# A dense layer with GELU, forward and backward: a shorter identity matrix, first loads on other queues, and all lists of operations written anew

## The chip, the core and the metric

The kernel runs on one core of a Trainium2 chip. A core has a matrix engine (TensorE, PE in the profile; its weight loads are shown apart as PEld), a vector engine (VectorE, DVE), a scalar engine (ScalarE, ACT), a general engine (GpSimd, POOL), and SyncE (SP), which here only issues transfers. Transfers run on 16 DMA engines. The metric is the device time of one execution in microseconds; three executions of the kernel before took 265.57 to 265.78 us, with a median of 265.76 us.

## What is computed

The reference is the forward pass and all gradients of a two-layer block with S = 2048 rows, D = 448 and F = 1792, in bf16:

```
h   = gelu_tanh(x @ w1 + b1)          # 2048 x 1792
out = h @ w2 + b2                     # 2048 x 448
gh  = (g @ w2.T) * gelu_tanh'(x @ w1 + b1)
gx  = gh @ w1.T    gw1 = x.T @ gh     gb1 = sum over rows of gh
gw2 = h.T @ g      gb2 = sum over rows of g
```

The outputs are out, gx, gw1, gb1, gw2 and gb2.

## The kernel before, in words

The rows are cut into 4 blocks of 512 and the 1792 hidden columns into 7 pairs of 128-column tiles, so there are 28 units called pairs, p = 0 to 27 (block p // 7). For a pair, TensorE makes `u` = x @ w1 (operations `u{p}.1` and `u{p}.2`, the two directions in which 64-row halves of the array are paired) and `q` = g @ w2.T (`q{p}.1`, `q{p}.2`). Between them and the results stand, for each pair: two copies of u out of PSUM with the bias added (`c{p}A`, `c{p}B`, on ScalarE or VectorE), the GELU and the square on ScalarE (`g`, `s`), six operations on VectorE (`e`, `r`, `y`, `z`, `m`, `n`) around a tanh on ScalarE (`t`), and last `G{p}` on VectorE, which multiplies by q and writes gh. There is one pair of PSUM banks for q, so q of the next pair waits for `G` of this one. The units `p`, `o` and `x` are the products h @ w2 and gh @ w1.T: `p{c}.{i}` makes a part of block 0's output from pair c, and `o{b}.{half}.{f0}.{f1}.{d}` and `x{b}.{half}.{f0}.{f1}.{d}` make half of block b over the hidden tiles f0 to f1. Their results are taken from PSUM by `vo` and `vx` on VectorE or ScalarE. After the last block come gw1 (line 775) and gw2 (line 829), each a run of full 128-row matmuls.

The order on each engine is written out by hand in `PE_ORDER`, `ACT_ORDER`, `DVE_ORDER` and `SP_ORDER`; a `Plan` links readers with writers and emits each engine's list in that order, so an engine that waits holds up all that is behind it. `UB` says which buffer holds u of a pair.

The start matters for the change. TensorE first runs six matmuls on a constant (`W6`). The first 512 rows of x come by plain transfers as three pieces: `xr01` is rows 0 to 127, `xr12` rows 128 to 255, and `xr24` rows 256 to 511. TensorE turns them by a matmul with an identity matrix (`X0` to `X3` on TensorE, line 574), and `X0`, `X2` on VectorE and `X1`, `X3` on ScalarE copy the turned rows out (line 581). The identity is made by `identity()` on VectorE: it counts along the columns by doubling, transposes the counts in 32x32 blocks, and compares counts and transposed counts in the four blocks on the diagonal of a tile that GpSimd set to zero. `b1T` on VectorE turns the bias b1. The first pair's u is made in halves of 256 rows (`h0.1`, `h0.2`, then `h1.1`, `h1.2`).

w1's main part comes in four parts by columns (`L0` 256 columns, `L1`, `L2`, `L3` 512 each), its last 128 rows in three (`Z0`, `Z1`, `Z2`), and two more pieces of it as `F` and `R`. `K0` to `K3` are the parts of w2, `K2` those of pairs 2 and 3. `X1` to `X3`, `Y0` to `Y3` and `J0` to `J3` in `SP_ORDER` are transfers that transpose: x and g of a block, and w2. Every transfer takes one of eight semaphores in turn (`DMAHW0` to `DMAHW7`), and the ninth is issued only when the first has landed.

Of the kernel before, what the change touches and what calls it, by code (L numbers as in the profile page):

```python
# [116 lines left out]
ident X0 b1T X2 b2c c0B0 c0B1 c1A c1B e0 r0 y0 c2A z0 e1 c3B c4B r1 e2 y1 r2 z1 c5B z2 y2 c6B m0 n0 m1 n1 c7B m2 Dg0
n2 c8B G0 e3 r3 c9B z3 y3 G1 vo0.2 m3 vo0.3 vo0.0 vo0.1 n3 G2 e4 c11B r4 e5 z4 r5 y4 z5 G3 m4 e6 n4 r6 y5 z6 y6 c13B
m5 G4 m6 n5 n6 e7 r7 y7 z7 G5 m7 vo1.0 vo1.1 n7 vo1.2 vo1.3 G6 e8 e9 r8 r9 z8 c14B z9 y8 y9 G7 m8 m9 n8 n9 e10 r10 y10
z10 G8 m10 e11 n10 r11 y11 z11 G9 m11 e12 n11 r12 y12 z12 G10 m12 e13 n12 r13 vx0.0 z13 y13 G11 c19B m13 e14 n13 r14  # L120
y14 z14 c20B G12 m14 e15 n14 r15 y15 z15 G13 m15 e16 n15 r16 y16 z16 G14 m16 e17 n16 r17 y17 c21B z17 G15 m17 vo2.0
vo2.1 c22B n17 vo2.2 vo2.3 G16 e18 e19 r18 c23B r19 z18 z19 y18 G17 y19 m18 e20 n18 m19 r20 n19 z20 G18 y20 e21 r21
y21 m20 c24B z21 n20 m21 G19 n21 e22 vx1.2 r22 y22 z22 c25B G20 m22 e23 n22 r23 y23 z23 c26B G21 m23 e24 n23 r24 y24
z24 c27B G22 m24 e25 n24 r25 y25 z25 G23 m25 e26 vx2.2 r26 n25 z26 y26 G24 m26 e27 n26 r27 y27 z27 G25 m27 n27 G26
vo3.0 vo3.1 vo3.2 vo3.3 G27 vx3.1 vx3.3
# [3 lines left out]
T0 T1 H10 T2 H11 T3 H12 T4 H13 T5 So1.0 So1.1 T6 H14 T7 H15 T8 Y2 H16 X3 T9 H17 T10 Sx0.0 H18 T11 Sx0.1 H19 T12 H20  # L129
# [30 lines left out]
def make_plan(tc, ctx, x, w1, b1, w2, b2, grad_out, out_0, out_1, out_2, out_3, out_4, out_5):  # L160
    nc = tc.nc
    P = 128
    _, S, D = x.shape
# [392 lines left out]
    def identity():  # L556

        nc.vector.memset(nums[:, 0:1], 0.0)  # L558
        for i in range(5):
# [1 line left out]
            nc.vector.tensor_scalar(out=nums[:, n:2 * n], in0=nums[:, 0:n], scalar1=float(n), scalar2=None, op0=ALU.add)  # L561
        for i in range(4):
            q = slice(32 * i, 32 * i + 32)
            nc.vector.transpose(out=turned[q, :], in_=nums[q, :])  # L564
        for i in range(4):
            q = slice(32 * i, 32 * i + 32)
            nc.vector.tensor_tensor(out=ident[q, q], in0=nums[q, :], in1=turned[q, :], op=ALU.is_equal)  # L567
# [305 lines left out]
```

## Time and profile before

| | |
|---|---|
| median of 3 executions | 265.76 us |
| the profiled execution | 265.63 us |
| its span, first to last instruction | 263.9 us |
| TensorE busy | 259.9 us (98%) |
| VectorE busy | 205.4 us (78%) |
| ScalarE busy | 124.1 us (47%) |
| GpSimd busy | 14.5 us (5%) |
| moved by the DMA engines | 46.50 MB, 176 GB/s over the span |

The profile is of one execution. "Busy" is the time in which an engine worked, and a group of instructions is shown with its count, its busy time, the mean of one in ns, and the idle time before it with what ended that. The chain is the work that ended last, followed back from the last instruction. In the timeline a row shows start, length, engine, line, operation, the tile written and the tile read. A transfer's "us to landing" is from its issue to the last count on its semaphore.

### The profile page before, as it was taken

How to read it: one execution, taken by the hardware profiler on the slowest of the kernel's cores; microseconds unless marked ns; L12 is line 12 of the kernel's file. 1: busy time of each engine (PE TensorE's matmuls, PEld its weight loads, DVE VectorE, ACT ScalarE, POOL GpSimd, SP SyncE). 2: the span in 40 equal slices, each digit the busy share in tenths (PEclk: the TensorE clock that was granted, in tenths of full speed). 3: DMA queues.
4: the chain of work that ended last, by engine and by line, in shares of the span. 5: the costliest groups of instructions: out<-in, count | busy, mean ns of one | idle time of the engine just before them, and what ended most of it. 6: DMA issues, size and time to landing. Idle time of an engine off the chain costs nothing.

```text
span 263.9 us, 5349 instructions
## 1 busy us (share of the span) xinstructions
PE 259.9 (98%) x2181; PEld 187.4 (71%) x2181; DVE 205.4 (78%) x300; ACT 124.1 (47%) x156; POOL 14.5 (5%) x9
## 2 busy tenths in 40 slices
PE   8999999999999999999999999999999999999995
PEld 4457889999888888888888887765555555555554
DVE  6796699999999999999999985339999999311000
ACT  4699777845998946456875530011122111000001
POOL 1000000000000000000000000000000392400000
PEclk9999999999999999999999999999999999999999
DMA  6999969999999982584357972984898998997221
GB/s 189 294 227 180 214 119 179 253 334 201 288 205 200 216 209 50 171 184 80 99 132 173 288 130 56 250 210 100 175 239 168 135 192 177 146 223 185 70 72 35
DMA packets 120107, 46.50 MB, mean 176 GB/s; under 512 B 96671, under 2 KB 119825, under 8 KB 120082
## 3 DMA queue, kind: packets, MB, share of 16 engines
q1 hardware_dynamic: 119250, 45.64, 78.8%
q10 hardware_dynamic: 832, 0.51, 0.6%
q8 instruction: 17, 0.28, 0.5%
q14 instruction: 8, 0.07, 0.1%
HBM read 8.09 MB, written 14.28 MB: 85 GB/s over the span
## 4 chain that ended last, share of the span: by engine, by line
PE 97%; DVE 1%; issue 0%; ACT 0%
PE bank L240 48%; PE qb L240 17%; PE bank L775 16%; PE bank L829 16%; PE bank L574 1%; DVE st L561 0%; DVE st L564 0%; DVE st L567 0%; ACT w_sb L834 0%; PE qb L651 0%; DVE st L558 0%
## 5 line engine op out<-in xcount | busy, mean ns | idle before, releaser
L240 PEld LDWEIGHTS <-HG 64*128 64x128 bf16 x896 | 73.9, 94 | 14.6 <-POOLq L235 1.7
L240 PE MATMUL qb<-gT,w2Tf 64*128 64x512 bf16 x392 | 57.8, 376 | 0.0
L240 PE MATMUL bank<-xT,w1f 64*128 64x512 bf16 (+1 forms) x371 | 53.3, 370 | 0.0
L240 PE MATMUL bank<-w_sb,HG 64*128 64x448 bf16 x448 | 51.8, 349 | 0.0
L240 PE MATMUL bank<-w1T_sb,HG 64*128 64x448 bf16 x448 | 51.0, 349 | 0.0
L829 PE MATMUL bank<-w2Tf,HG 128*128 128x448 bf16 (+2 forms) x240 | 42.6, 340 | 0.0
L775 PE MATMUL bank<-w1f,gh_nat 128*128 128x448 bf16 x224 | 42.5, 353 | 0.0
L240 PEld LDWEIGHTS <-w2Tf 64*128 64x128 bf16 x392 | 35.3, 94 | 6.0 <-POOLq L235 0.5
L475 DVE SCALAR_TENSOR_TENSOR HG<-TR,qb 128x1024 bf16<-128x1024 bf16 x28 | 34.0, 1214 | 7.1 <-PE qb L240 7.1
L240 PEld LDWEIGHTS <-w1f 64*128 64x128 bf16 x382 | 31.3, 94 | 8.8 <-POOLq L235 1.5
L829 PEld LDWEIGHTS <-HG 128*128 128x128 bf16 x240 | 22.9, 98 | 19.8
L775 PEld LDWEIGHTS <-gh_nat 128*128 128x128 bf16 x224 | 21.8, 98 | 20.6 <-issue 0.4
L460 ACT ACTIVATE TR<-TR 128x1024 bf16<-128x1024 bf16 x28 | 29.3, 1050 | 9.7 <-DVE TR L450 9.6
L798 DVE TENSOR_TENSOR w1T_sb<-w1T_sb,gh_nat 128x1792 f32<-128x1792 f32 x14 | 28.4, 2026 | 0.5
L780 ACT ACTIVATE TR<-bank 128x448 bf16<-128x448 f32 x14 | 7.6, 543 | 34.9 <-PE bank L775 34.9
L835 DVE CAST w_sb<-bank 128x448 bf16<-128x448 f32 x6 | 3.7, 623 | 26.0 <-PE bank L829 26.0
L834 ACT CAST w_sb<-bank 128x448 bf16<-128x448 f32 (+2 forms) x9 | 4.4, 491 | 37.7 <-PE bank L829 37.7
L804 POOL PARTITION_ALL_REDUCE w1T_sb<-w1T_sb x1 | 10.7, 10661 | 207.4 <-DVE w1T_sb L802 207.4
L435 ACT ACTIVATE TR<-gh_nat 128x1024 bf16<-128x1024 bf16 x15 | 15.5, 1051 | 10.9 <-DVE TR L470 10.9
L465 DVE TENSOR_SCALAR TR<-TR 128x2048 bf16<-128x2048 bf16 x28 | 19.1, 685 | 1.8 <-ACT TR L460 1.7
L470 DVE TENSOR_TENSOR TR<-TR 128x1024 bf16<-128x1024 bf16 x28 | 19.0, 683 | 0.1
L455 DVE TENSOR_TENSOR TR<-TR,HG 128x1024 bf16<-128x1024 bf16 x28 | 19.0, 682 | 0.0
(49 smaller groups left out, 191.2 us busy)
## 6 DMA issues: line engine op xcount, KB each, us to landing
hT_dram<-HG SPq DMA_DIRECT2D x28, 256.0 KB, 3.4
out_dram<-st SPq DMA_DIRECT2D x16, 224.0 KB, 2.5
w1f<-in_x_dram SPq DMA_DIRECT2D x2, 896.0 KB, 8.5
w1f<-in_w_dram SPq DMA_DIRECT2D x3, 384.0 KB, 6.0
w2Tf<-in_grad_out_dram SPq DMA_DIRECT2D x2, 560.0 KB, 6.5
out_dram<-w_sb SPq DMA_DIRECT2D x2, 448.0 KB, 2.7
out_dram<-xT SPq DMA_DIRECT2D x2, 384.0 KB, 2.8
w_sb<-in_w_dram SPq DMA_DIRECT2D x1, 672.0 KB
```

What stands on the lines that cost most here:

```text
L240: m = nc.tensor.matmul(bk_(b)[:, 0:n], lhsT=l, rhs=r, start=st, stop=sp, skip_group_check=True)
L435: pl.op("ACT", f"s{p}", lambda: nc.scalar.activation(out=TR[p % NTR][:, 1], in_=ubuf(p), func=ACT.Square, scale=sc), [("ub", p)], [v], ("a ...
L455: pl.op("DVE", f"R{p}", lambda: nc.vector.tensor_tensor(out=t[:, 1], in0=t[:, 1], in1=hblk(p), op=ALU.mult), [("r", p), ("h", p)], [val((" ...
L460: pl.op("ACT", f"t{p}", lambda: nc.scalar.activation(out=t[:, 0], in_=t[:, 0], func=ACT.Tanh), [("y", p)], [val(("t", p), ("TR0", p % NTR) ...
L465: pl.op("DVE", f"m{p}", lambda: nc.vector.tensor_scalar(out=t[:], in0=t[:], scalar1=1.0, scalar2=None, op0=ALU.subtract), [("t", p), ("r2" ...
L470: pl.op("DVE", f"n{p}", lambda: nc.vector.tensor_tensor(out=t[:, 0], in0=t[:, 0], in1=t[:, 1], op=ALU.mult), [("m0", p), ("m1", p)], [val( ...
L475: pl.op("DVE", f"G{p}", lambda: nc.vector.scalar_tensor_tensor(out=ghblk(p), in0=t[:, 0], scalar=2.0, in1=qb[:, :, :], op0=ALU.subtract, o ...
L775: nc.tensor.matmul(bk_(bk)[:, 0:D], lhsT=gh_nat[:, st // 4, ft, st % 4, :], rhs=x_nat[:, st, :], start=(st == 0), stop=(st == NS - 1))
L780: fn = (lambda dst=dst, src=src: nc.scalar.mul(out=dst, in_=src, mul=-0.5)) if eng == "ACT" else \
L798: nc.vector.tensor_tensor(out=hs3, in0=a, in1=gh_nat[:, st // 4, :, st % 4, :], op=ALU.add)
L804: pl.op("POOL", "gb1", lambda: nc.gpsimd.partition_all_reduce(gb1_w, hsum, channels=P, reduce_op=bass_isa.ReduceOp.add), ["hsc"], ["gb1"], ...
L829: nc.tensor.matmul(bk_(bk)[:, 0:d1 - d0], lhsT=h_nat[ft][:, st, :], rhs=g_nat[:, st, d0:d1], start=(st == 0), stop=(st == NS - 1))
```

## The change

`identity()` now takes nine operations on VectorE's queue: one memset, four doublings (counts 0 to 15), one operation that makes 128 counts out of 8 x 16, one transpose of all 128 partitions, one addition of the partition block's offset, and one comparison over the whole 128x128 tile. GpSimd, which set the identity's tile to zero as the last of its three memsets, now writes the four block offsets as its first work, by four memsets of 32 partitions.

In `SP_ORDER` the loads `L0` and `L1` follow directly on `xr01` and `xr24`, and `Z1` follows them; `b1` and `b2` go to ScalarE's queue behind `xr12` and `Z0`. Before, ScalarE's queue had `L0`, `Z0` and `Z1`. `K1` now follows `L3` (before, `K0`), `R` goes ahead of `L3`, and `Y0` (the transposing load of g's first block) goes ahead of `J0` (that of w2's first part).

The lists are written anew after that. The hidden tiles of `o` and `x` are cut at 6 and 10 (before: 5 and 10). `q0.1` and `q0.2` stand directly behind `u8.1` and `u8.2`. The copies `c5A`, `c6A`, `c7A`, `c10B` and `c12B` and the evictions `vx0.2`, `vx0.3`, `vx1.0`, `vx2.1` and `vx2.3` go from ScalarE to VectorE, `c5B`, `c19B`, `c21B`, `c22B`, `vx1.2` and `vx2.2` from VectorE to ScalarE, and others change places within a list. `UB` goes round ten buffers where it went round fourteen.

```diff
 PE_ORDER = """
 ...
-p1.2 p1.3 u6.1 p2.0 u6.2 p2.1 p2.2 p2.3 p3.0 p3.1 p3.2 u7.1 p3.3 u7.2 p4.0 p4.1 p4.2 p4.3 p5.0 p5.1 u8.1 p5.2 u8.2
-q0.1 p5.3 q0.2 u9.1 p6.0 u9.2 q1.1 p6.1 q1.2 u10.1 p6.2 u10.2 q2.1 p6.3 q2.2 u11.1 o1.1.0.5.1 u11.2 q3.1 o1.0.0.5.1
+p1.2 p1.3 u6.1 p2.0 u6.2 p2.1 p2.2 p2.3 p3.0 p3.1 p3.2 u7.1 p3.3 u7.2 p4.0 p4.1 p4.2 p4.3 p5.0 p5.1 u8.1 q0.1 u8.2
+q0.2 p5.2 u9.1 p5.3 u9.2 q1.1 p6.0 q1.2 u10.1 p6.1 u10.2 p6.2 q2.1 p6.3 q2.2 u11.1 o1.1.0.6.1 u11.2 q3.1 o1.0.0.6.1
 ...
 ACT_ORDER = """
-xr12 L0 Z0 Z1 table X1 X3 c0A0 c0A1 s0 g0 s1 c2B c3A s2 c4A g1 g2 g3 c5A g4 g5 t0 c6A t1 g6 s3 s4 c7A t2 g7 c8A s5 g8
+xr12 Z0 b1 b2 table X1 X3 c0A0 c0A1 s0 g0 s1 c2B c3A s2 c4A g1 g2 g3 c5B g4 g5 t0 t1 g6 t2 s3 s4 g7 s5 c8A g8 c9A t3
 ...
 SP_ORDER = """
-xr01 xr24 b1 b2 L1 L2 Z2 K0 K1 F L3 R K3 K2 X1 J0 Y0 J1 I0 J2 Y1 E J3 I1 So0.1 X2 So0.0 H0 H1 H2 H3 H4 H5 H6 H7 H8 H9
+xr01 xr24 L0 L1 Z1 Z2 L2 K0 F R L3 K1 K3 K2 X1 Y0 J0 J1 I0 J2 Y1 E J3 I1 X2 So0.1 So0.0 H0 H1 H2 H3 H4 H5 H6 H7 H8 H9
 ...
-UB = (0, 1, 2, 3, 4, 5, 6, 7, 8, 9, 10, 11, 12, 13, 0, 1, 2, 3, 4, 5, 6, 0, 1, 2, 0, 1, 2, 0)
+UB = (0, 1, 2, 3, 4, 5, 6, 7, 8, 9, 0, 1, 2, 3, 4, 5, 6, 7, 8, 9, 0, 1, 2, 0, 1, 2, 0, 1)
 ...
-    nums, turned = stage[1][:, 0, 0:32], stage[1][:, 0, 32:64]
+    nums, turned, nums128 = stage[1][:, 0, 0:16], stage[1][:, 0, 32:64], stage[1][:, 0, 128:256]
+    row, block = [stage[1][:, 1, 2 * i:2 * i + 2].bitcast(F32) for i in (0, 1)]
 ...
-        for i in range(5):
+        for i in range(4):
             n = 1 << i
             nc.vector.tensor_scalar(out=nums[:, n:2 * n], in0=nums[:, 0:n], scalar1=float(n), scalar2=None, op0=ALU.add)
-        for i in range(4):
-            q = slice(32 * i, 32 * i + 32)
-            nc.vector.transpose(out=turned[q, :], in_=nums[q, :])
-        for i in range(4):
-            q = slice(32 * i, 32 * i + 32)
-            nc.vector.tensor_tensor(out=ident[q, q], in0=nums[q, :], in1=turned[q, :], op=ALU.is_equal)
+        low = nums[:, None, 0:16].to_broadcast([P, 8, 16])
+        high = nums[:, 0:8, None].to_broadcast([P, 8, 16])
+        nc.vector.scalar_tensor_tensor(out=nums128.rearrange("p (a b) -> p a b", a=8), in0=high, scalar=16.0, in1=low, op0=ALU.mult, op1=ALU.add)
+        nc.vector.transpose(out=turned, in_=nums128[:, 0:32])
+        nc.vector.tensor_scalar(out=row, in0=turned[:, 0:1], scalar1=block, scalar2=None, op0=ALU.add)
+        nc.vector.tensor_scalar(out=ident, in0=nums128, scalar1=row, scalar2=None, op0=ALU.is_equal)
 ...
+    def blocks():
+        for i in range(4):
+            nc.gpsimd.memset(block[32 * i:32 * i + 32, :], 32.0 * i)
+
+    pl.op("POOL", "identz", blocks, [], ["identz"], ("tiny", 1))
     pl.op("POOL", "b1z", lambda: nc.gpsimd.memset(b1n[:], 0.0), [], ["b1z"], ("tiny", 1))
     pl.op("POOL", "b2z", lambda: nc.gpsimd.memset(stage[NST - 1][0:64, 0, :], 0.0), [], ["b2z"], ("tiny", 1))
-    pl.op("POOL", "identz", lambda: nc.gpsimd.memset(ident, 0.0), [], ["identz"], ("tiny", 1))
```

VectorE at the start, from the first doubling to the first copy of turned x (`st_82` holds the counts, `st_81` the identity, `xT` the turned x). Before:

```order
L561 TENSOR_SCALAR st_82<-st_82 128x8 [waits DVE_49]
L561 TENSOR_SCALAR st_82<-st_82 128x16 [waits DVE_49]
L564 STREAM_TRANSPOSE st_82<-st_82 32x32 [waits DVE_49]
L564 STREAM_TRANSPOSE st_82<-st_82 32x32 x3
L567 TENSOR_TENSOR st_81<-st_82 32x32 [waits DVE_49,Pool_49]
L567 TENSOR_TENSOR st_81<-st_82 32x32 [waits DVE_49] x3
L581 CAST xT_68<-bank_89 128x4x128 [waits PE_49]
```

Now:

```order
L562 TENSOR_SCALAR st_82<-st_82 128x8 [waits DVE_49]
L565 SCALAR_TENSOR_TENSOR st_82<-st_82 128x128 [waits DVE_49]
L566 STREAM_TRANSPOSE st_82<-st_82 128x32 [waits DVE_49]
L567 TENSOR_SCALAR st_82<-st_82 128x1 [waits DVE_49,Pool_49]
L568 TENSOR_SCALAR st_81<-st_82 128x128 [waits DVE_49]
L582 CAST xT_68<-bank_89 128x4x128 [waits PE_49]
```

Nine operations between the fourth doubling and the copy have become four.

SyncE's first transfers, in the order in which it issues them (`TR` holds rows of x, `b1n` and `st` the biases, `w1f` and `gh_nat` parts of w1, `w_sb` parts of w2; a `DMAHW` wait is for an earlier transfer's landing). Before:

```order
L516 DMA TR_80<-in_x_dram 128x448
L516 DMA TR_80<-in_x_dram 128x2x448
L516 DMA b1n<-in_b_dram 14x128 [waits Pool_49]
L516 DMA st_83<-in_b_dram 1x448 [waits Pool_49]
L516 DMA w1f<-in_w_dram 128x3x512 [waits DMAHW0_49]
L516 DMA w1f<-in_w_dram 128x3x512 [waits DMAHW1_49]
L516 DMA gh_nat<-in_w_dram 128x1024 [waits DMAHW2_49]
```

Now:

```order
L516 DMA TR_80<-in_x_dram 128x448
L516 DMA TR_80<-in_x_dram 128x2x448
L516 DMA w1f<-in_w_dram 128x3x256
L516 DMA w1f<-in_w_dram 128x3x512
L516 DMA gh_nat<-in_w_dram 128x512 [waits DMAHW0_49]
L516 DMA gh_nat<-in_w_dram 128x1024 [waits DMAHW1_49]
L516 DMA w1f<-in_w_dram 128x3x512 [waits DMAHW2_49]
```

`L0` and `L1` are now the third and fourth transfer and wait for no landing; before, `L1` was the fifth and waited for `DMAHW0`, the semaphore of `xr12`.

TensorE at the end of `u8.1` (`xT_69` with `w1f`) and what follows: `p5.2` reads `HG`, and `q0.1` reads `w2Tf` and `gT_70`. Before:

```order
L240 LDWEIGHTS w1f
L240 MATMUL bank_93<-xT_69,w1f 128x512
L240 LDWEIGHTS HG [waits Pool_sequencer_49]
L240 MATMUL bank_92<-w_sb,HG 128x448
L240 LDWEIGHTS HG
L240 MATMUL bank_91<-w_sb,HG 128x448
```

Now:

```order
L240 LDWEIGHTS w1f
L240 MATMUL bank_93<-xT_69,w1f 128x512
L240 LDWEIGHTS w2Tf [waits DMAHW4_49]
L240 MATMUL qb<-gT_70,w2Tf 128x512 [waits DMAHW3_49]
L240 LDWEIGHTS w2Tf
L240 MATMUL qb<-gT_70,w2Tf 128x512
```

The first use of `J0`'s and `Y0`'s data has moved ahead of `p5.2` and `u8.2`, and of the two loads the one of w2 is now issued second.

More of the change, by code (lines that the diff above doesn't have):

```diff
@@ L108 @@
+x3.1.6.10.1 x3.0.6.10.2 x3.1.6.10.2 x3.0.10.14.1 x3.1.10.14.1 x3.0.10.14.2 x3.1.10.14.2
 """
 ACT_ORDER = """
-xr12 L0 Z0 Z1 table X1 X3 c0A0 c0A1 s0 g0 s1 c2B c3A s2 c4A g1 g2 g3 c5A g4 g5 t0 c6A t1 g6 s3 s4 c7A t2 g7 c8A s5 g8
-c9A g9 t3 c10A c10B g10 s6 c11A g11 t4 c12A c12B g12 s7 t5 c13A t6 g13 s8 s9 t7 s10 c14A g14 t8 t9 c15A c15B g15 s11
-s12 t10 c16A c16B g16 s13 t11 c17A c17B g17 s14 t12 c18A c18B g18 s15 vx0.1 t13 c19A vx0.2 vx0.3 g19 s16 c20A t14 g20
-s17 t15 s18 t16 s19 c21A t17 g21 c22A g22 s20 c23A g23 t18 t19 s21 s22 t20 c24A t21 g24 s23 vx1.0 vx1.1 s24 vx1.3 c25A
@@ L115 @@
+c26A g26 s26 c27A t24 g27 s27 vx2.0 vx2.2 t25 t26 t27 vx3.0 vx3.2
 """
 DVE_ORDER = """
[L117 to L125, printed above, removed]
+ident X0 b1T X2 b2c c0B0 c0B1 c1A c1B e0 r0 y0 c2A z0 e1 c3B c4B r1 e2 y1 r2 z1 c5A z2 y2 c6A c6B m0 m1 n0 n1 m2 c7A
@@ new lines @@
+c7B n2 Dg0 c8B G0 e3 r3 y3 c9B z3 m3 G1 n3 c10B vo0.2 vo0.3 vo0.0 vo0.1 G2 e4 e5 c11B r4 r5 z4 z5 y4 G3 c12B m4 e6 n4
+r6 y5 z6 c13B m5 G4 n5 e7 y6 r7 y7 z7 m6 G5 m7 vo1.0 vo1.1 n6 vo1.2 vo1.3 n7 G6 e8 e9 r8 r9 c14B z8 z9 y8 y9 G7 m8 m9
+n8 n9 e10 r10 y10 z10 G8 m10 e11 n10 r11 y11 z11 G9 m11 e12 n11 r12 y12 z12 G10 m12 vx0.0 n12 e13 vx0.2 r13 vx0.3 z13
+G11 y13 e14 r14 y14 z14 m13 m14 c20B n13 n14 G12 e15 r15 y15 z15 m15 G13 n15 e16 r16 y16 z16 G14 m16 vo2.0 vo2.1 n16
+vo2.2 vo2.3 e17 G15 r17 e18 z17 r18 y17 z18 G16 m17 e19 n17 r19 y18 z19 y19 G17 m18 m19 n18 n19 e20 r20 G18 z20 e21
@@ L126 @@
+y20 r21 c23B z21 vx1.0 m20 G19 n20 e22 y21 r22 c24B z22 y22 m21 G20 c25B m22 n21 n22 e23 r23 y23 z23 c26B m23 G21 n23
+e24 r24 y24 z24 c27B m24 n24 G22 vx2.1 e25 vx2.3 r25 y25 z25 G23 m25 e26 n25 r26 y26 z26 G24 m26 e27 n26 r27 y27 z27
+G25 m27 n27 vo3.0 vo3.1 G26 vo3.2 vo3.3 G27 vx3.1 vx3.3
 """
 SP_ORDER = """
[L128 to L129 removed]
```

34 lines of the change are left out of this document (18 added, 16 removed).

## The prediction

> **What bounds the kernel now.** I read first what TensorE waits for, then the chain that ended last, then the timeline of the first ten microseconds, and last the transfers. TensorE's own wait after its first instruction (time, number, longest):
>
> ```profile
> PE bank L574 <- DVE st L567: 0.5, 1, 0.5
> ```
>
> Pieces of the chain (start, length, what):
>
> ```profile
> 3.99 1.80 PE bank L574 x16
> ...
> 10.63 0.86 PE qb L240 x8
> ...
> 218.79 42.43 PE bank L829 x240
> 261.24 0.27 ACT w_sb L834
> ```
>
> The wait on line 567, the identity, is the only one that the matmuls themselves show, and from 3.99 to 261.24 the chain is TensorE without a gap worth naming. So the end moves by what the start moves, less every new stall behind it. Busy time by stretch (columns: stretch, length, PE, PEld, DVE, ACT and POOL busy with counts, clock, DMA share, GB/s):
>
> ```profile
> 4.60:5.75 1.15, 1.15 (x14) 1.02 (x14) 1.09 (x3) 0.58 (x1) 0.00 (x0) 1.00 0.68 129
> 5.75:9.30 3.55, 3.54 (x44) 1.83 (x44) 2.26 (x6) 1.41 (x3) 0.00 (x0) 1.00 1.02 343
> 29.21:89.30 60.09, 60.09 (x592) 53.23 (x589) 57.68 (x95) 46.66 (x56) 0.00 (x0) 1.00 1.02 223
> ```
>
> Two things follow: the DMA engines run at 129 GB/s between 4.60 and 5.75 and at 343 right after, so loads have a hole there; and from 29.21 to 89.30 VectorE is busy 57.68 of 60.09 us, so it has little room. The start in the timeline:
>
> ```profile
> 0.76 2.72 PE L366 MATMUL qb<-const-bfloat16-1.0 128*128 128x512 bf16 x6 [0.76 <-PEq L857]
> 0.89 1.22 DVE L561 TENSOR_SCALAR st<-st 128x1 bf16<-128x1 bf16 x5
> 2.15 0.91 DVE L564 STREAM_TRANSPOSE st<-st 32x32 bf16<-32x32 bf16 x4
> 3.08 0.76 DVE L567 TENSOR_TENSOR st<-st 32x32 bf16<-32x32 bf16 x4
> 3.41 0.93 SPq L516 DMA_DIRECT2D w1f<-in_w_dram  x2
> 4.61 0.69 DVE L581 CAST xT<-bank 128x512 bf16<-128x512 f32 x1 [0.77 <-PE bank L574]
> 5.33 0.85 DVE L670 STREAM_TRANSPOSE b1T<-b1n 32x32 bf16<-32x32 bf16 x4
> 5.72 0.50 PE L240 MATMUL bank<-xT,w1f 64*128 64x256 bf16 x6
> 6.21 0.69 DVE L581 CAST xT<-bank 128x512 bf16<-128x512 f32 x1
> 6.45 0.50 PE L240 MATMUL bank<-xT,w1f 64*128 64x256 bf16 x5
> 6.96 0.50 PE L240 MATMUL bank<-xT,w1f 64*128 64x256 bf16 x6
> 7.55 0.82 PE L240 MATMUL bank<-xT,w1f 64*128 64x512 bf16 x6
> ```
>
> The rows on PE from 5.72 on are `h0.1`, `h0.2`, `h1.1` and `u1.1`. In the list of waits for this time `h1.1` waits for the copy of `X2` (6.21 + 0.69 = 6.90) and `u1.1` for a part of w1, `L1`:
>
> ```profile
> PEld L240 <- DVE xT L581: 0.3, 1, 0.3
> PEld L240 <- DMA w1f<-in_w_dram: 0.3, 1, 0.3
> ```
>
> **The change, part by part. The identity.** The mean of one operation:
>
> ```profile
> L475 DVE SCALAR_TENSOR_TENSOR HG<-TR,qb 128x1024 bf16<-128x1024 bf16 x28 | 34.0, 1214 | 7.1 <-PE qb L240 7.1
> L561 DVE TENSOR_SCALAR st<-st 128x1 bf16<-128x1 bf16 (+4 forms) x5 | 1.1, 217 | 0.2
> L564 DVE STREAM_TRANSPOSE st<-st 32x32 bf16<-32x32 bf16 x4 | 0.8, 203 | 0.1
> L567 DVE TENSOR_TENSOR st<-st 32x32 bf16<-32x32 bf16 x4 | 0.7, 167 | 0.1
> ```
>
> Four doublings end at about 1.9 (0.89 + 1.22 less the last, 0.2). The three-operand operation over 128 elements has no row; it lies between 0.17 (32 elements) and 1.21 (1024), and on the line through both it takes 0.27. The transpose over 128 partitions lies between 0.20 (one of 32) and 0.91 (four); I take 0.20, since the partitions of a row's operation run side by side in every other row. The two scalar operations take 0.22 each. With three hundredths between operations the identity is ready at 1.9 + 0.91 + 0.12 = 2.9 instead of 3.84; with the upper ends it is 4.7, with the lower 2.8. GpSimd's four small memsets lie beside the doublings, and the offsets are wanted only at 2.5.
>
> **The first matmul.** With the identity at 2.9, `X0` is held by `W6`, which ends at 0.76 + 2.72 = 3.48, and by `xr12`: SyncE issued `L1` at 3.41, the moment `xr12`'s semaphore came free. So `X0` starts at about 3.46 instead of 3.99: 0.53 earlier, not 0.95. Next late is `xr24`, wanted by `X2` at 3.46 + 0.86 = 4.32:
>
> ```profile
> TR<-in_x_dram SPq DMA_DIRECT2D x1, 224.0 KB, 3.5
> w1f<-in_w_dram ACTq DMA_DIRECT2D x1, 192.0 KB, 3.8
> ```
>
> Both were issued near 1.16 and shared the engines, landing at 4.6 and 4.9. Now `L0` (192 KB) queues behind `xr24` on one ring and only `Z0` (64 KB) runs beside it. 128 KB less in front at 343 GB/s is 0.4, so `xr24` lands near 4.2. `L0` then ends about as before, 4.7 to 5.2, when `h0.1` wants it. If `xr24` stays at 4.6, `X2` waits 0.3, of which 0.1 is hidden by VectorE's chain below.
>
> **Up to `u1.1`.** From `X0` VectorE runs copy, `b1T`, copy: 3.99 to 6.90 before, 2.91 long, so it ends at 6.37 now, if `b1` is there by 4.8 (it follows 176 KB on ScalarE's ring). TensorE: `X0` to `X3` end at 3.46 + 1.80 = 5.26, `h0.1` to the end of `h0.2` took 6.45 - 5.72 and three steps of 0.107, which ends at 6.3, or at 6.5 with the slow clock below. So `h1.1` starts at 6.43 to 6.5 instead of 6.96 (0.49 gained in the middle). Its four steps took 0.107 each (below), so they ended at 7.4, while `u1.1` started at 7.55: 0.11 went on `L1`. `L1` is now issued near 2, not 3.41, and follows `L0` on its ring: 384 KB at 343 GB/s are 1.15, so it lands near 6; `Z1` (issued at 3.41, when `xr12` has landed) follows it by 128 KB, 0.4. Both are there before 6.9. So `u1.1` starts 0.60 earlier.
>
> The slow clock: `X0` to `X3` took 1.80/16 = 0.112 for 128 columns each, while in the chain at 10.63 four steps of 512 columns took 0.86, which is 0.107 for 256. `h0.1` and the one matmul behind it fit into 6.45 - 5.72 = 0.73 only at the second pace, so the matrix clock doubled near 5.6. If it keeps that place, nearly 0.4 us of `h0.1` now run at half speed and cost 0.2, which is in the 6.5 above. The Trainium skill (TensorE: Matmul & The Clock Gate, Part 1: The HAM clock gate) has the clock released by a free-running window of about 3.4 us, so that closing the gap before `X0` could also bring the release one window forward. By that rule the start would gain about 0.2 more; by the row it gains 0.60. I take the row, one execution though it is.
>
> **The other loads.** Without the hole the loads come (343 - 129) x 1.15 / 343 = 0.7 earlier. That has to hold where the margin is small:
>
> ```profile
> w_sb<-in_w_dram SPq DMA_DIRECT2D x1, 448.0 KB, 10.6
> w2Tf<-in_w_dram SPq DMA_TRANSPOSE x1, 4.9
> gT<-in_grad_out_dram SPq DMA_TRANSPOSE x1, 6.9
> ```
>
> ```profile
> 8.11 1.28 SPq L516 DMA_DIRECT2D w_sb<-in_w_dram  x2
> 9.43 9.83 SPq L528 DMA_TRANSPOSE xT<-in_x_dram  x1
> 19.31 1.29 SPq L528 DMA_TRANSPOSE w2Tf<-in_w_dram  x1
> 20.64 3.12 SPq L528 DMA_TRANSPOSE gT<-in_grad_out_dram  x1
> ```
>
> ```profile
> 19.52 0.72 PE L240 MATMUL bank<-w_sb,HG 64*128 64x448 bf16 x4
> 27.07 0.91 PE L240 MATMUL bank<-xT,w1f 64*128 64x512 bf16 x6
> 28.96 0.91 PE L240 MATMUL qb<-gT,w2Tf 64*128 64x512 bf16 x6
> ```
>
> `K2`, the second transfer of its row (8.75), landed at 19.3 and `p2.0` used it at 19.52. Now `p2.0` comes at 18.92 and `K2` at 18.6. `J0` and `Y0` landed at 24.2 and 27.5 and `q0.1` used both at 28.96. Now `q0.1` stands right behind `u8.1` (27.07 + 0.65), so at 27.72 - 0.60 = 27.12, and the two loads, swapped but the same bytes, end at 27.5 - 0.7 = 26.8. Margins of 0.3 both. `K1` and `L3` change places with `R`, of like size, and had more room. I cost these at nothing; the cover is those margins, and what exceeds them comes out at the end in full.
>
> **The lists.** The cuts at 6 leave the number of matmuls as it is (448 for out and gx each), so cost nothing on TensorE. `UB` reuses a buffer ten pairs later; pair 0's reader ends near 13 and `c10` comes past 33: nothing. ScalarE is not close to full. VectorE is:
>
> ```profile
> L412 DVE TENSOR_SCALAR gh_nat<-bank,b1T 128x512 bf16<-128x512 f32 x10 | 7.5, 747 | 2.1 <-PE bank L240 1.7
> L503 DVE TENSOR_SCALAR st<-bank 128x448 bf16<-128x448 f32 x5 | 3.1, 623 | 8.1 <-PE bank L240 7.9
> ```
>
> In 29 to 89 it gains `c10B`, `c12B`, `vx0.2`, `vx0.3` and loses `c19B`: 2 x 0.75 + 2 x 0.62 - 0.75 = 2.0 against 60.09 - 57.68 = 2.4 idle. I cost it at nothing because the new list on TensorE puts the `q` from 12 on further back, among `o` and `x` work that waits for nothing; without that cover the bound is 2.0.
>
> **Sum.** 0.49 + 0.11 = 0.60 earlier, all of it carried to the end: 265.63 - 0.60 = 265.03 on the profiled execution, which is 0.13 under the median, so 265.15 for the median.
>
> **The rivals.** (a) The loads do not come forward, because the hole only moves: then `p2.0` starts at 19.35 to 19.45 and the gain left is 0.1, or 265.65. For it: `K2` and the transposing load behind it, whose issue alone lasted 9.83, show that the DMA engines are the slower part up to 20. Against it: the hole has a visible cause, the wait of `L1` at 3.41. Half of it gives 265.4. That the identity gets no shorter can be too: at its upper-end prices `X0` starts at 4.7, 0.7 later than before, or 266.4; no row shows a transpose or a 128-element operation that slow. (b) The other side: VectorE becomes the bound between 29 and 89. If its 2.4 us idle can't be used, since it waits there for q from TensorE (7.1 us in the row of line 475), `G` is late and each next `q` with it; up to 2.0 - 0.60 = 1.4 slower, 267.15. It decides once over 1.13 of the 2.0 come through. (c) `J0` behind `Y0` lands later than the pair did: one more transposing issue of 1.29 would put it at 28.8, stall `q0.1` by 1.7 and give 266.85; slower from a landing past 28.2.
>
> **Numbers.** 0.2% is 0.53 us, about what a measurement of this kernel tells from no change. Forecast 48%, from 264.85 (the extra 0.2 of the clock) to 265.23. (a) 30%, from there to 265.7. (b) 10% and (c) 8%, half of each past the bound of slower, half short of it; the rest, 4%, is the slow identity. Faster 0.48, same 0.30 + 0.09 = 0.39, slower 0.09 + 0.04 = 0.13. The range reaches from 264.85 into the first part of (b) and (c): 265.9.
>
> **What would show it.** The identity's last operation ends near 2.9 and `X0` starts near 3.46; `h1.1` near 6.45 with no wait for `L1`; `p2.0` near 18.9 and `q0.1` near 27.1, without an idle PE before them; gw1 begins near 175.7 instead of 176.31. I am wrong if TensorE's waits show a transfer near 19 or 27, or a `G` on line 475 between 29 and 89.

## The result, and the profile after

The changed kernel takes 266.35 us in the median of 14 executions (265.51 to 267.59), the kernel before 265.69 (265.47 to 265.95): a ratio of 1.0032, with an interval of 1.0016 to 1.0048. It is slower by 0.3%, and outside the range that was given. Timed twice more, later, the same kernel gave 265.74 (ratio 1.0004, 0.9989 to 1.0018) and 265.62 (1.0002, 0.9991 to 1.0014): no difference from the kernel before. None of the three shows the 0.6 us that was forecast. What is common to them is the spread: single executions reach 266.9 to 267.6, which the kernel before does in one of 146. Three executions in the experiments, in which TensorE was throttled for a part or nearly all of the run (979.5, 394.9 and 275.4 us), are left out of all medians and ranges.

Its profiled execution took 265.84 us, span 264.1. The chain of work that ended last (start, length, what) no longer begins with the identity on VectorE, but with a transfer of w1:

```profile
1.63 4.40 DMA w1f<-in_w_dram
6.88 0.87 PE bank L240 x14
7.76 2.01 PE bank L240 x20
9.80 1.04 PE bank L240 x8
...
176.54 42.48 PE bank L780 x224
219.02 42.43 PE bank L834 x240
```

The transfer of 1.63 to 6.03 is `L0`. In the chain of the kernel before, the pieces at `u2.1` and at gw1 are these:

```profile
9.59 1.04 PE bank L240 x8
...
176.31 42.48 PE bank L775 x224
```

From the piece at `u2.1` to gw1 it is 166.72 us before and 166.74 after. So in this profile the lists, the later loads and the whole middle cost and gain nothing on balance; the 0.21 us by which the profile is later stand at 9.6 us already. The start in the timeline of after (start, length, engine, line, operation, tiles, idle time before it):

```profile
2.14 0.29 DVE L565 SCALAR_TENSOR_TENSOR st<-st 128x128 bf16<-128x128 bf16 x1
2.46 0.21 DVE L566 STREAM_TRANSPOSE st<-st 128x32 bf16<-128x32 bf16 x1
2.79 0.21 DVE L567 TENSOR_SCALAR st<-st 128x1 f32<-128x1 bf16 x1
3.04 0.26 DVE L568 TENSOR_SCALAR st<-st 128x128 bf16<-128x128 bf16 x1
3.35 2.16 PE L575 MATMUL bank<-st,TR 128*128 128x128 bf16 x16
6.08 0.50 PE L240 MATMUL bank<-xT,w1f 64*128 64x256 bf16 x6 [0.57 <-DMA w1f<-in_w_dram]
7.15 0.49 PE L240 MATMUL bank<-xT,w1f 64*128 64x256 bf16 x6
7.76 0.33 PEld L240 LDWEIGHTS <-w1f 64*128 64x128 bf16 x6 [0.29 <-DMA w1f<-in_w_dram]
9.80 0.82 PE L240 MATMUL bank<-xT,w1f 64*128 64x512 bf16 x6
10.66 0.83 PE L240 MATMUL qb<-xT,w1f 64*128 64x512 bf16 x6
```

`X0` starts 0.64 us earlier than before (3.35 for 3.99), `h0.1` 0.36 later (6.08 for 5.72), because it waits 0.57 us for `L0`; `u1.1` waits for `L1` as it did before. The row of `L0` among the transfers (size, us from issue to landing), which had 3.8 on ScalarE's queue:

```profile
w1f<-in_w_dram SPq DMA_DIRECT2D x1, 192.0 KB, 4.4
```

It was issued 0.47 us later than before and took 0.6 longer: it landed at 6.04 instead of 4.92. The 16 parts of a transfer land one by one on its semaphore, and the trace has each: those of `L0` came from 4.20 to 4.92 before, and from 4.48 to 6.04 after, ten of them by 4.70. The stretch with little transferred is still there in this profile (busy time of PE, PEld, DVE, ACT, POOL, then clock, DMA share, GB/s):

```profile
4.00:5.00 1.00, 0.88 (x10) 0.62 (x8) 0.99 (x3) 0.74 (x2) 0.00 (x0) 1.00 0.81 171
5.00:6.00 1.00, 0.51 (x5) 0.24 (x3) 0.94 (x4) 0.46 (x1) 0.00 (x0) 1.00 1.02 310
```

Before, the same two stretches were these:

```profile
4.00:5.00 1.00, 1.00 (x10) 1.00 (x11) 0.39 (x1) 0.19 (x1) 0.00 (x0) 1.00 0.88 245
5.00:6.00 1.00, 1.00 (x15) 0.85 (x14) 0.93 (x5) 0.76 (x2) 0.00 (x0) 1.00 0.76 170
```

Here the hole did not close when `L1` was issued earlier; it came earlier. But it isn't what makes `L0` late: in the second profile of the same kernel (`e4_again` below) the two stretches were these, and `L0` landed at 5.86 all the same:

```profile
4.00:5.00 1.00, 0.81 (x12) 0.59 (x10) 0.90 (x3) 0.74 (x2) 0.00 (x0) 1.00 0.93 268
5.00:6.00 1.00, 0.26 (x6) 0.10 (x4) 0.94 (x4) 0.59 (x1) 0.00 (x0) 1.00 1.02 332
```

In the first profile ten packets of 512 and 1024 bytes took 370 to 800 ns between 4 and 6 us, where most take 27 to 46; the kernel before has eight of 350 to 820 ns there, from 4.86 on, when all of `L0` but its last part had landed.

### The profile page after: what moved, and what is told of

Its sections match the earlier page's. It is cut to its first block, busy times and chain, and to the rows that moved or that the text cites. A ratio compares the mean times of both kernels' runs of the same rounds, so it can differ in the third digit from the quotient of the medians.

```text
span 264.1 us, 5355 instructions
## 1 busy us (share of the span) xinstructions
PE 259.9 (98%) x2181; PEld 158.7 (60%) x2181; DVE 207.3 (79%) x299; ACT 123.0 (47%) x152; POOL 14.6 (6%) x12
## 4 chain that ended last, share of the span: by engine, by line
PE 97%; DMA 2%; SPq 0%; issue 0%; ACT 0%
PE bank L240 48%; PE qb L240 17%; PE bank L780 16%; PE bank L834 16%; DMA w1f<-in_w_dram 2%; SPq L516 0%; ACT w_sb L839 0%; PE qb L652 0%
## 5 line engine op out<-in xcount | busy, mean ns | idle before, releaser
L240 PEld LDWEIGHTS <-HG 64*128 64x128 bf16 x896 | 60.2, 94 | 27.9 <-POOLq L235 1.5
L240 PE MATMUL qb<-gT,w2Tf 64*128 64x512 bf16 x392 | 53.6, 376 | 0.0
L240 PE MATMUL bank<-xT,w1f 64*128 64x512 bf16 (+1 forms) x371 | 49.8, 370 | 0.6 <-DMA w1f<-in_w_dram 0.6
L240 PE MATMUL bank<-w_sb,HG 64*128 64x448 bf16 x448 | 49.1, 349 | 0.0
L240 PE MATMUL bank<-w1T_sb,HG 64*128 64x448 bf16 x448 | 48.5, 349 | 0.0
L240 PEld LDWEIGHTS <-w2Tf 64*128 64x128 bf16 x392 | 26.5, 94 | 13.9 <-POOLq L235 0.3
L240 PEld LDWEIGHTS <-w1f 64*128 64x128 bf16 x382 | 23.9, 94 | 16.7 <-DMA w1f<-in_w_dram 1.3
L435 ACT ACTIVATE TR<-gh_nat 128x1024 bf16<-128x1024 bf16 x14 | 14.5, 1050 | 8.2 <-DVE TR L470 8.2
```

What stands on the lines that cost most here:

```text
L240: m = nc.tensor.matmul(bk_(b)[:, 0:n], lhsT=l, rhs=r, start=st, stop=sp, skip_group_check=True)
L435: pl.op("ACT", f"s{p}", lambda: nc.scalar.activation(out=TR[p % NTR][:, 1], in_=ubuf(p), func=ACT.Square, scale=sc), [("ub", p)], [v], ("a ...
```

## The experiments

The change has three parts that can be taken singly: the identity, the heads of the load lists, and the rest of the lists with `UB`. All experiments together are in one table at the end of this section. The expectations call an engine's queue of transfers its ring.

**The three parts singly, and the whole again.** The first kernel is before with the new identity:

```diff
-        for i in range(5):
+        for i in range(4):
 ...
-            nc.vector.transpose(out=turned[q, :], in_=nums[q, :])
+        nc.vector.transpose(out=turned, in_=nums128[:, 0:32])
 ...
-            nc.vector.tensor_tensor(out=ident[q, q], in0=nums[q, :], in1=turned[q, :], op=ALU.is_equal)
+        nc.vector.tensor_scalar(out=ident, in0=nums128, scalar1=row, scalar2=None, op0=ALU.is_equal)
```

> The kernel before with only the new identity. Theory L (the loss and the scatter come from the order of the first loads): X0 starts near 3.4, but u1.1 still waits for L1, which lands near 7.5, so the time stays within 0.2 us of before (265.5 to 265.8) and the executions lie as close together as before, within 0.5 us. Theory S (the new lists lose time where VectorE has no room): the same here, since the lists are the old ones.

The second is before with the new heads of the load lists alone:

```diff
-xr12 L0 Z0 Z1 table
+xr12 Z0 b1 b2 table
 ...
-xr01 xr24 b1 b2 L1 L2 Z2 K0 K1 F L3 R K3 K2 X1
+xr01 xr24 L0 L1 Z1 Z2 L2 K0 F R L3 K1 K3 K2 X1
```

> The kernel before with only the new order of the loads up to the first transposing one, on SyncE and ScalarE. Theory L: h0.1 waits for L0, which lands near 6.0 instead of 4.9, the time is 0.2 to 1.0 us above before, and the executions scatter by more than 1 us. Theory S: as before or 0.1 faster, no scatter.

The third is before with all else of the new lists, behind before's heads of the load lists:

```diff
-UB = (0, 1, 2, 3, 4, 5, 6, 7, 8, 9, 10, 11, 12, 13, 0, 1, 2, 3, 4, 5, 6, 0, 1, 2, 0, 1, 2, 0)
+UB = (0, 1, 2, 3, 4, 5, 6, 7, 8, 9, 0, 1, 2, 3, 4, 5, 6, 7, 8, 9, 0, 1, 2, 0, 1, 2, 0, 1)
 ...
```

> The kernel before with the new lists behind the first loads (and the new use of buffers), old identity and old first loads. Theory L: within 0.2 us of before, executions within 0.5 us. Theory S: 0.5 to 0.8 us above before, executions scatter by 1 to 2 us.

The fourth is the whole change, unedited.

> The changed kernel once more, for a second profile. Theory L: L0 lands at a different time than 6.0, h0.1 starts right behind it, and everything behind is shifted by the same amount. Theory S: h0.1 starts near 6.1 again and a difference in time opens between 29 and 176.

None of the three parts alone differs from before (0.9995, 1.0005 and 1.0003, and 1 lies in all three intervals). The loss that theory L expected of the heads did not come, and neither did its cause: `L0` landed at 5.08 there, not near 6.0. The identity alone brings `h0.1` to 5.03, 0.69 us earlier, and has lost it at `u1.1`:

```profile
5.03 0.50 PE L240 MATMUL bank<-xT,w1f 64*128 64x256 bf16 x6
...
7.66 0.82 PE L240 MATMUL bank<-xT,w1f 64*128 64x512 bf16 x6 [0.46 <-DMA w1f<-in_w_dram]
```

`L1` landed at 7.62. So with before's loads the identity is worth nothing that can be measured, since `L1` comes when it comes. The new lists alone cost nothing.

**In pairs.** Two theories stood then: the start decides (S, a letter that stood for the lists in the first four expectations), or the new lists run into something in the middle in some executions (T).

> The new identity with the new heads of the load lists, and before's four instruction lists. Theory S (the start decides: the work from u2.1 on takes the same time in every profile so far, gw1's first matmul 166.64 to 166.67 us behind u2.1, and u2.1 itself waits for L1 or L2, so the time is the landing of L0, L1 and L2 and nothing else): 265.3 to 265.9 in the median, the same sum from u2.1 to gw1 (166.6 to 166.7, or 0.3 more where L2 lands after 10.2), and among the executions some above 266.9 us, as the whole change has (6 of 22), since the new loads are in it. Theory T (the new lists leave TensorE no room in the middle, and in some executions something there comes late): nothing above 266.7, as for the loads alone (highest 266.7).

> The new identity with the new lists, and before's loads (L0 on ScalarE's ring behind xr12, L1 fifth on SyncE's ring). Theory S: h0.1 near 5.0 as with the identity alone (L0 lands at 4.7), u1.1 at L1's landing (7.5 to 7.8), so 265.5 to 265.9 us, no execution above 266.6. Theory T: the new lists are in it, so some executions above 266.9 us.

> The new loads with the new lists, and before's identity of 15 operations (ready at 3.84 us). Theory S: L0 at 5.0 to 6.1, u1.1 at 7.4 to 7.8, 265.5 to 266.0 us in the median, and executions above 266.9 where L0 and L1 come late. Theory T: the same spread, since the lists are in it; only a spread as narrow as before's (265.4 to 266.2) would speak against both, and for the identity as a part of it.

> The whole change a third time, for its spread beside the three pairs on one chip, and for one more profile. Both theories: median 265.7 to 266.4, one execution in four above 266.9. Where the profile is of such an execution, theory S expects u2.1 a whole microsecond later (10.5 to 11.5, behind L1 or L2) and gw1 166.7 us after it; theory T expects u2.1 at 9.4 to 9.9 and a wait of TensorE of more than 1 us between 12 and 176 us.

Every profile at full clock agreed with S (one of the four, of the identity and the heads, was the throttled execution of 979.5 us), but late executions, above 266.9 us, came with loads and lists together (4 of 12) and not with the loads and the identity (0 of 10), as T has it. That needed a profile of a late execution, for which three more profiles were taken, and a version with `L0` back on ScalarE's ring:

```diff
-xr12 Z0 b1 b2 table
+xr12 L0 Z0 b1 b2 table
 ...
-xr01 xr24 L0 L1 Z1 Z2 L2 K0 F R L3 K1 K3 K2 X1
+xr01 xr24 L1 Z1 Z2 L2 K0 F R L3 K1 K3 K2 X1
```

> The whole change, but with the loads' heads mixed: ScalarE's ring takes xr12 L0 Z0 b1 b2, SyncE's xr01 xr24 L1 Z1 Z2 L2 K0 and the rest as in the change. L0 goes back to where it was issued at 1.16 us, L1 is issued third on SyncE's ring (1.63) instead of fifth. Theory S (start-bound: L0, L1 and L2 decide, one after the other): L0 lands at 4.7 to 5.0, h0.1 starts at 5.0 to 5.4, L1 at 6.5 to 7.0, u1.1 at 6.6 to 7.1, u2.1 at 8.9 to 9.2 unless L2 (9.5 to 10.2) holds u3.1; 264.9 to 265.4 us in the median. Theory T (the lists cause the late executions): the same early gain in the profile, yet some executions above 266.9 us.

> New loads with new lists and before's identity once more, for a profile of a late execution (4 of 12 of this kernel were above 266.9). If it is one: theory S expects L1 or L2 to land 1 us or more later than the 6.99 and 10.03 us of the run before and u2.1 with it, and 166.7 us from u2.1 to gw1; theory T expects u2.1 near 9.3 and a wait of TensorE of more than 1 us between 12 and 176 us. If it is none, it gives one more landing of L0 (5.1 to 6.0), L1 (6.9 to 7.7) and L2 (9.9 to 10.5).

> The same kernel and the same question again: in a late execution theory S has u2.1 late by L1 or L2 and 166.7 us from there to gw1, theory T has u2.1 near 9.3 and a wait of TensorE of more than 1 us behind it.

> The whole change, the same question: in a late execution theory S has u2.1 late by L1 or L2 and 166.7 us from there to gw1, theory T has u2.1 near 9.4 and a wait of TensorE of more than 1 us behind it.

The mixed heads took 267.48 instead of the 265 that was expected. `L0` and `L1` landed as expected (4.96, 6.73), but `b1`, issued at 2.22 behind `L0` and `Z0`, landed only at 6.53, and VectorE turns it ahead of the copy of `X2`. Its chain of work:

```profile
2.22 4.31 DMA b1n<-in_b_dram
...
7.27 0.20 DVE b1T L675
7.48 0.03 issue
7.51 0.70 DVE xT L582
8.21 0.04 issue
8.25 2.45 PE bank L240 x28
```

The first of the three profiles met a late execution, 267.31 us. `L0`, `L1` and `L2` are no later than in the others (5.93, 7.22, 9.56), and from `u3.1` to the end it takes as long as everywhere. What is different is TensorE's pace. The rows of `u1.1` and the one behind it in the late execution:

```profile
8.60 1.43 PE L240 MATMUL bank<-xT,w1f 64*128 64x512 bf16 x6
9.83 0.41 PE L240 MATMUL bank<-xT,gh_nat 64*128 64x512 bf16 x2
10.05 0.42 PE L240 MATMUL bank<-xT,w1f 64*128 64x256 bf16 x4
```

and in the next profile, the same kernel at 265.76 us:

```profile
7.56 0.81 PE L240 MATMUL bank<-xT,w1f 64*128 64x512 bf16 x6
8.21 0.38 PE L240 MATMUL bank<-xT,gh_nat 64*128 64x512 bf16 x2
8.42 0.49 PE L240 MATMUL bank<-xT,w1f 64*128 64x256 bf16 x5
```

From `u1.1` to the next half it is 1.45 us instead of 0.86. The trace's record of the granted clock has its first entry, at full speed, at 9.78 us in the late one and at 5.14 in the other. Ahead of that entry it is empty (the clock column of the stretches shows 1.00 there too), but the paces of the matmuls show half speed: in the late execution those of 512 columns follow one another at 0.427 us ahead of 9.78 and at 0.216 behind it. In the 15 other profiles with six matmuls ahead of `X0` that have such a record the release comes at 3.84 to 6.75, although the first matmul starts at 0.76 in each, and then the full clock holds for 259.413 us in all but one (262.826), and for 256.000 in this one. These are 76, 77 and 75 times 3.4133 us. So there is a window of 3.413 us that runs on by itself, the clock is released at one of its ends, and in the late execution the end at 6.37 (9.78 less 3.41) passed without a release. The Trainium skill (TensorE: Matmul & The Clock Gate, Part 1: The HAM clock gate) states just this, a free-running window of 3413 ns, and a release after a busy window; here the trace agrees. What the wait for `L0` had to do with it isn't shown: ahead of `X0` TensorE was idle for 0.50 us here as in the kernel before, and ahead of `h0.1` for 0.13.

**The clock, put to the test.** Theory C: TensorE's idle time ahead of `h0.1` makes a window too empty. The first kernel, the whole change with two matmuls more, fills it; the second empties the windows of the kernel before; the third, before's lists with the new identity, takes the wait away by other places in the rings:

```diff
-W6 X0 X1 X2 X3 h0.1
+W6 X0 X1 X2 X3 W2 h0.1
```

> The whole change with two matmuls of ones (128 x 512, results never read) put between X3 and h0.1, where TensorE waits 0.4 to 1.0 us for L0. Theory C (the late executions are those in which TensorE's idle time ahead of h0.1 makes the clock's release miss one boundary of 3.41 us): no execution above 266.9, and a median of 265.6 to 265.8, since h0.1 waits for L0 as before and the filler costs at most 0.2. Theory D (late executions come from L0, L1 or L2 themselves): the same spread as without the filler, some executions at 266.9 to 267.6.

```diff
-W6 X0 X1 X2 X3 h0.1
+W2 X0 X1 X2 X3 h0.1
```

> The kernel before with two matmuls ahead of X0 (W2) instead of six (W6): the work that is left out computes nothing, and X0 waits for the identity until 3.99 us as before. Theory C: the window that ends between 4 and 6.8 us holds too little work, the clock comes free at 6.8 to 10.2 us, one boundary later in most executions, and they take 266.3 to 267.4 us where before takes 265.7. Theory D: the loads are untouched, so 265.6 to 265.8 as before.

```diff
-xr12 L0 Z0 Z1 table
+xr12 L0 Z0 table
 ...
-xr01 xr24 b1 b2 L1 L2 Z2 K0 K1 F L3 R K3 K2 X1
+xr01 xr24 b1 b2 L1 Z1 L2 Z2 K0 K1 F L3 R K3 K2 X1
```

> The new identity with before's lists and other load heads: ScalarE's ring takes xr12 L0 Z0, SyncE's xr01 xr24 b1 b2 L1 Z1 L2 Z2 and then before's order. L0 lands at 4.7 to 5.0 as it does on ScalarE's ring, L1 is the eighth transfer of all, so it needs no semaphore of an earlier one (issue near 2.7 instead of 3.41). Both theories: h0.1 at 5.0 to 5.4, u1.1 at 6.8 to 7.2 behind L1 and Z1, u2.1 at 8.9 to 9.2, 265.0 to 265.4 us and no execution above 266.5. If L1 lands no earlier than 7.4, the transfers and not the issue set it, and the time is 265.5 to 265.8.

With two matmuls ahead of `X0` the kernel before, its loads as they were, takes 266.43 (265.84 to 267.21; 1.0021, 1.0006 to 1.0035), and its profile has the clock released at 8.88. `u1.1`, now at half pace in its first part:

```profile
8.40 1.09 PE L240 MATMUL bank<-xT,w1f 64*128 64x512 bf16 x6
```

The window that ended at 5.47 without a release (8.88 less 3.41) has 1.49 us of matrix work. So too little matrix work in a window costs a release, without any change of a load. The filled kernel had no execution above 266.42 in 11. This is weak: 15 of 82 executions of the kernels with the new heads were above 266.9, and at that rate 11 without one come up once in ten times.

**What was left.** The last three runs asked whether before's lists protect from late executions, and whether the new version could be mended: its profile had lost 0.8 us at `p2.0`, to `K2`.

```profile
9.15 10.78 DMA w_sb<-in_w_dram
19.98 9.52 PE bank L240 x94
```

```diff
-xr01 xr24 b1 b2 L1 Z1 L2 Z2 K0 K1 F L3 R K3 K2 X1
+xr01 xr24 b1 b2 L1 Z1 L2 Z2 K0 K1 F L3 K3 K2 R X1
```

> The kernel of e15 with R issued behind K2 instead of ahead of K3. If K2's landing is what e15's profile lost 0.8 us on at p2.0: K2 lands 0.3 to 0.5 us earlier, no wait of TensorE near 19 us, 265.0 to 265.3 us in the median, gw1 166.7 us behind u2.1. If the transposing load X1 or Y0 is what is late then (Y0 landed at 27.8 there), the time stays at 265.26 or the wait moves to q0.1 near 29.

> The new identity and the new loads with before's lists again. Theory C: L0 lands at 5.1 to 6.0, and one execution in four or five is above 266.7, by chance none so far. If the lists had a part in it: L0 near 5.1 to 5.5 again and no execution above 266.7.

> The new loads alone once more, for the landing of L0: theory C expects 5.1 to 6.0 as in the other kernels with these loads; if before's lists brought it forward, 5.0 to 5.5.

`K2` landed at 18.23 instead of 19.94 and nothing waited for it any more (the time behind the start of `u3.1` is 255.17 us, as elsewhere); the median stayed where it was, which suggests that it had been late in few executions.

With before's lists, the new identity and the new heads 3 of 12 were above 267.4, the profiled one (267.54) among them. So a late execution doesn't need the new lists, and in no profile does it come from the middle: theory T falls. Whether the lists make late executions more frequent stays open: 12 of 48 were above 266.9 with the new lists and heads, and 3 of 34 with the new heads and before's lists. But this profile is not late by the clock, which came free at 3.87. It is late by `L2` (chain, and TensorE's waits: total, times, longest):

```profile
4.33 7.98 DMA w1f<-in_w_dram
12.35 1.04 PE qb L240 x8
```

```profile
PE qb L240 <- DMA w1f<-in_w_dram: 2.0, 1, 2.0
```

Its 16 parts landed from 7.94 to 12.31, nine by 8.54; before they came from 7.57 to 8.68. In the last profile, with the heads alone, `L0` came at 4.92 and `L2` at 11.00 us. That is earlier than theory C expected, and the lists seem to have a part in it: with the new heads `L0` landed at 4.92 to 5.48 in the four profiles with before's lists and at 5.47 to 6.04 in the eight with the new ones, though the lists first differ behind these loads. Why is open. So there are two causes of late executions, the clock and `L2`. With six matmuls ahead of `X0` the profiles show both with the new heads only; but the heads alone had no late execution in 12, and the one of the kernel before (267.17) was not profiled.

How many fall to each cause isn't known from one profile of each, and no late execution of the whole change was profiled. The mean granted clock of an execution gives a hint: it is 0.994 in two of the 15 (267.59 and 267.53) and in the three of the mixed heads above 268 us, and half speed for one window of 3.413 us out of 265.8 would make it 0.9936. It doesn't settle it: in the late profile above it is 1.000, since the half speed lies ahead of the record's first entry.

All runs; times in us; the landings, the release of the clock and the start of `u3.1` are of the profiled execution, and the last column is its time less that start (a blank stands where the record of the clock is empty or the profiled execution was throttled):

| kernel | median (lowest to highest) | `L0`, `L1`, `L2` | clock | `u3.1` | rest |
|---|---|---|---|---|---|
| before | 265.69 (265.47 to 265.95) | 4.92, 7.50, 8.68 | 5.58 | 10.45 | 255.18 |
| after | 266.35 (265.51 to 267.59) | 6.04, 7.71, 10.49 | 5.46 | 10.66 | 255.17 |
| identity alone | 265.58 (265.34 to 265.91) | 4.66, 7.62, 8.62 | 4.55 | 10.57 | 255.16 |
| heads alone | 265.71 (265.36 to 266.70) | 5.08, 7.40, 10.02 | 4.37 | 10.35 | 255.20 |
| lists alone | 265.82 (265.35 to 266.51) | 4.72, 7.78, 8.87 | 6.50 | 10.73 | 255.21 |
| after, second | 265.74 (265.04 to 267.17) | 5.86, 6.87, 10.51 | 4.19 | 10.56 | 255.20 |
| identity, heads | 266.00 (265.34 to 266.69) | 5.48, 7.69, 10.85 | | | |
| identity, lists | 265.71 (265.39 to 266.25) | 4.82, 7.65, 8.73 | 5.46 | 10.60 | 255.19 |
| heads, lists | 266.24 (265.32 to 267.58) | 5.66, 6.99, 10.03 | 3.84 | 10.10 | 255.22 |
| after, third | 265.62 (265.35 to 266.91) | 5.79, 6.88, 9.88 | 5.63 | 10.23 | 255.23 |
| mixed heads | 267.48 (266.65 to 268.35) | 4.96, 6.73, 10.37 | 6.19 | 11.59 | 255.20 |
| heads, lists: one execution | 267.31 | 5.93, 7.22, 9.56 | 9.78 | 12.12 | 255.19 |
| heads, lists: one execution | 265.76 | 6.01, 7.08, 10.52 | 5.14 | 10.56 | 255.20 |
| after: one execution | 265.67 | 6.01, 7.05, 10.19 | | 10.45 | 255.22 |
| after, filled | 265.90 (265.70 to 266.42) | 5.47, 7.08, 10.59 | 5.91 | 10.63 | 255.20 |
| before, `W2` | 266.43 (265.84 to 267.21) | 4.70, 7.51, 8.57 | 8.88 | 11.57 | 255.18 |
| `L1` ahead | 265.26 (264.95 to 266.45) | 4.66, 6.75, 9.14 | 4.16 | 9.91 | 256.00 |
| and `R` behind `K2` | 265.35 (265.07 to 265.97) | 4.65, 6.76, 9.04 | | 10.18 | 255.17 |
| identity, heads again | 266.01 (265.23 to 267.54) | 5.47, 7.25, 12.31 | 3.87 | 12.35 | 255.19 |
| heads alone: one execution | 266.23 | 4.92, 7.60, 11.00 | 6.75 | 11.04 | 255.19 |

The last column is the main result: in all profiles but one, with old lists or new, the time is the start of `u3.1` and 255.2 us. The exception is the profile that lost 0.8 at `p2.0`. `u3.1` is the first row on `qb` that reads `w1f`: after it is the row at 10.66 in the timeline above, and before it is this one:

```profile
10.45 0.83 PE L240 MATMUL qb<-xT,w1f 64*128 64x512 bf16 x6
```

The loads are in three groups: with before's heads `L0` lands at 4.7 to 4.9, `L1` at 7.5 to 7.8, `L2` at 8.6 to 8.9; with the new heads at 4.9 to 6.0, 6.9 to 7.7 and 9.6 to 12.3; with `L1` eighth of all and `Z1` and `Z2` each behind the part that is wanted first, at 4.7, 6.8 and 9.0 to 9.1.

The two versions of the last group, with the new identity and the old lists, are faster than the kernel before, if barely: 0.9982 (0.9967 to 0.9997) and 0.9988 (0.9979 to 0.9997). Their medians lie below all three of the changed kernel too.

## Why the prediction was wrong, point by point

- **The identity and `X0`**: ready at 3.30 instead of 2.9, since the doublings ended at 2.11 (taken as 1.9) and the four operations behind them took up to 0.29 us with gaps of up to 0.12 between them. One doubling alone took 0.61; it ended 0.03 after GpSimd's memset for `b2` (1.41 to 1.87), which the four new memsets had moved back, and in the kernel before the one doubling of 0.42 us ends 0.03 after a memset too. Whether the memset holds it up wasn't tried. `X0` started at 3.35, where 3.46 was said, but the reason given was wrong: `X0` doesn't wait for `xr12`, which landed at 3.40; the last thing that it waited for was the identity. The lateness of the identity cost at most 0.08 us, because the last of `W6`'s matmuls starts at 2.85 and they follow one another at 0.427. That part of the number is luck. (The upper end of the identity, given as 4.7, adds up to 4.6.)
- **`xr24`**: 4.43 instead of 4.2, and `X2` waited 0.3, as the sentence on that case had it.
- **The step that failed: "`L0` then ends about as before, 4.7 to 5.2".** It landed at 6.04, in other profiles at 4.92 to 6.01. Its landing was set by the bytes ahead of it over a mean rate. But a transfer is there when its last part is there: ten of `L0`'s sixteen came by 4.70, the others up to 1.3 us later. That `L1`, now issued 0.5 us behind it, held them up is a guess: with the heads alone, which have the same loads, `L0` landed at 5.08 and 4.92.
- **`L1` near 6**: 7.71, by the same mistake, and 6.87 or later in every profile with the new heads. Its wait, which the sum let go, stayed (0.29 us in the profile). In effect this is near rival (a), loads that do not come forward, but at `h0.1` and `u1.1`, where the sum had no margin to lose, and not at `p2.0`, where the prediction looked for it.
- **`L2`, put at nothing without a word**: by the forecast `u3.1` starts at 10.45 - 0.60 = 9.85. `L2` landed at 8.68 before, and at 9.88 to 12.31 in all but one of the twelve profiles with the new heads (9.56 in that one). So even with `L0` and `L1` on time the gain would have met `L2`; in six of these profiles `u3.1` waits for it.
- **The clock**: "if it keeps that place, I take the row". In this profile it did (5.46 for 5.58). But one execution's row was no place: in the profiles the release falls anywhere over 2.9 us, and in one late execution a whole window more was lost. The window of the rule that was set aside is there; that closing the gap ahead of `X0` brings the release forward, as it could have done by that rule, no run shows, and the price that was seen is upward.
- **The other loads**: forward, as forecast and by more. `K2` landed at 17.9 (19.3 before), `Y0` and `J0` at 22.6 and 24.2, so `p2.0` and `q0.1` waited for no transfer, and rival (c) did not come. None of the waits that the prediction named as signs of being wrong came either; the waits were at `h0.1` and `u1.1`.
- **The lists at nothing**: right for everything behind `u3.1`, by the column of the rest; whether they have a part in the landing of `L0` is open. Rival (b) did not come.
- **The sum**: 0.60 earlier was forecast at `u1.1`; it is 0.21 later there in the profile, all from `L0` and `L1`. (A slip beside it: the range begins at 264.85, where 265.15 less the 0.2 of the clock is 264.95.) What puts the first median another 0.5 us up is the spread of the executions, for which the prediction had no term: five of the 14 were above 266.9, and the median of the other nine is 266.16. Why there were more late ones then than later (1 of 8, 1 of 11) stays open.

## What to carry to other kernels

An operation on the critical path that gets shorter gains only up to the next transfer, so the landing of each early load has to be set against its first use, one by one. Several loads in flight are not a line that moves at the mean rate: each waits for its slowest part, and every load up to the point where the start ends needs its own line in the sum. Small ones that an engine needs early, such as a bias, go ahead of large ones. And gaps in TensorE's work at the start can keep the clock at half speed for a window longer.

## What the runs showed of the hardware

- The matrix clock is released at an end of a window of 3.413 us that does not start with the kernel: at 3.84 to 6.75 us over 15 profiles, and at 8.88 and 9.78 where one end of a window had passed without a release. In the window that failed in the late profile (2.95 to 6.37) TensorE was busy for 81%, in one that released (the kernel with the lists alone, 3.09 to 6.50) for 85%. One release came after a window with 80% (heads and lists, 0.42 to 3.84), so the busy share alone does not decide it; whether some matmuls count for less wasn't tried.
- The 16 parts of one transfer land up to 4.4 us apart. From the first part to the last it was 0.3 to 1.7 us for `L0` (192 KB), 1.2 to 2.1 for `L1` and 1.3 to 4.4 for `L2` (384 KB each) with the new heads, and 0.3 to 0.7, 1.0 to 1.4 and 1.0 to 1.2 with before's heads.
- A bias of 14 x 128 took 4.31 us to land behind two parts of w1 on its ring, and 2.8 to 3.7 where it had one part or none ahead of it there.
